# Attention in units of all eight heads, with the row maxima subtracted on GpSimd and one exponential of the transposed scores

## The chip, the cores and the metric

The kernel runs on one core of a Trainium2 chip. Its time is the device time of one execution in microseconds (us). The core has five engines that run their own instruction streams and meet at semaphores: TensorE (PE in the profile, with PEld for its weight loads), VectorE (DVE), ScalarE (ACT), GpSimd (POOL) and SyncE (SP), which issues most of the transfers (DMA). Inputs and outputs lie in HBM, tiles in SBUF, and products of TensorE in PSUM, which GpSimd cannot read.

## The reference

Windowed attention, and behind it an expert layer in which a greedy routing gives each of 8 experts 576 of the 4608 tokens. The change concerns the attention alone, and some constants of the routing.

```python
# q, k, v: (8 batches, 8 heads, 576 tokens, 64)
scores = (q @ k^T) / 8
mask   = 0 <= query - key < 64          # a query sees itself and 63 keys before it
scores = where(mask, scores, -1e9)
scores = scores - max(scores, axis=-1)
attn   = exp(scores) / (sum(exp(scores)) + 1e-9)
x      = (attn @ v)                      # 4608 tokens x (8 heads * 64) = the experts' input
logits = x @ w_gate                      # 8 numbers for each token: greedy choice, 576 tokens for each expert
out[tokens of e] = relu(x[tokens of e] @ w1[e]) @ w2[e]
```

## The kernel before, in words

Tokens are cut into blocks of 64 queries, nine for each batch; a block needs only the 128 keys of its own block and the one before it. Two blocks that follow each other (`a` = 0, 1) make a unit `m` of 128 queries, so there are 36 units, and a unit can reach over the end of a batch. A step of the loop at line 248 works on half a unit: four of the eight heads (`g` = 0, 1), 72 half-units in all, in a pipeline that is written out by hand. A half-unit goes through these stages, one step apart:

- `qk` (line 116): 16 products of TensorE, 64 rows by 64 columns each, into the two PSUM tiles `Sp` of this `g`. Behind them VectorE makes for each head one instruction (line 135) that adds the mask (an SBUF tile) to the PSUM scores, writes the result, negated and scaled, to `st`, and keeps its minimum in `mx`; a second small instruction (DVE_READ_ACCUMULATOR) writes that minimum out. Between the four heads stand the pieces of `norm` of the half-unit four steps back.
- `sm` (line 141): four exponentials on ScalarE, one for each head, since each head's maximum goes in as the per-row bias.
- `tr` (line 148): four 128x128 transposes on TensorE into the PSUM tile `Tp`, and one copy by ScalarE to `pt`.
- `pv` (line 164): 16 products of TensorE, 128 rows by 64 columns each, `pt` times the values, into `Op`. The value tile has 73 columns for each head: 64 values, 8 columns of the head's gate logits, and one column of ones that gives the row sum.
- `norm` (line 177): VectorE adds 1e-9 to the row sums (line 203), takes the reciprocal (204), and scales the gate columns (188) and the values (198). After every fourth unit it sums the gate logits over the heads (192).

Blocks with an even number need keys in an order that the value tile `VO` doesn't have on its partitions; `even` (line 109) copies two halves of each into `VE`, on GpSimd (the first two on VectorE). The gate columns come from products of `vt` with the gate's weights, made for each batch in two parts: `gate_mm` on TensorE, `gate_cp` on ScalarE, `gate_tr` (transposes) on TensorE, `gate_out` on VectorE (lines 80 to 107), which writes them into `VO` and so waits until `v` of that batch has landed.

The order on each engine is the order in which the code is written, and the table `at` says in which step the gate's pieces, the even blocks and the loads of a later batch are put. TensorE's order in a step is `qk(s)`, `tr(s-2)`, `pv(s-3)`, then gate work. All inputs and stores of the attention go through SP's queue, in order; the loads of batches 0 and 1 come first, that of batch b in the middle of batch b-2. Finished units `x` are held back (up to 16) and stored to `xs` later. Between the steps VectorE also runs pieces of the routing: `setup` builds its constants, one or three pieces for each step, and `late` makes each token's best choice once its logits are there. The routing's rounds and the experts follow when the attention is over, and are the same in both kernels.

Of the kernel before, what the change touches and what calls it, by code (L numbers as in the profile page):

```python
# [9 lines left out]
FT = mybir.dt.float32  # L10
# [16 lines left out]
HOLD = 16  # L27
# [3 lines left out]
def attention(ctx, tc, c, q, k, v, vt, gate, xs, L, choices, setup, counters):  # L31
# [48 lines left out]
    def gate_mm(b, i0, i1):  # L80
        if not i0:
            VS[b] = [None, wk.tile([128, S], FT, name="vs", bufs=2)]
        pv = VS[b][0] = ps.tile([128, 512], FT, name="pvt", bufs=1)
        for p in range(HP):
            nc.tensor.matmul(pv[32 * p:32 * p + 32, :64 * (i1 - i0)], wgbd[:, p, :],
                             VT[b][:, p, 64 * i0:64 * i1], start=True, stop=True)
# [2 lines left out]
        nc.scalar.activation(VS[b][1][:, 64 * i0:64 * i1], VS[b][0][:, :64 * (i1 - i0)], AF.Copy)  # L89

    def gate_tr(b, i0, i1):
        pt = VS[b][0] = ps.tile([128, 512], FT, name="pvt", bufs=1)
        for n, j in enumerate(range(i0 // 2, (i1 + 1) // 2)):
            w = 128 if j < 4 else 64
            nc.tensor.transpose(pt[:w, 128 * n:128 * n + 128], VS[b][1][:, 128 * j:128 * j + w], c["ident"])

    def gate_out(b, i0, i1):
        pt = VS[b][0]
        j0, j1 = i0 // 2, i1 // 2
        n = j1 - j0  # L100
        nc.vector.tensor_copy(VO[b][:, j0:j1, :, 64:72],
                              pt[:, :128 * n].rearrange("p (j h g) -> p j h g", j=n, h=8)[:, :, :, :8])
        if i1 % 2:
            nc.vector.tensor_copy(VO[b][0:64, 4, :, 64:72],
                                  pt[:64, 128 * n:128 * n + 128].rearrange("p (h g) -> p h g", h=8)[:, :, :8])
        if not i0:
            VE[b] = ld.tile([128, 4, H, VW], FT, name="VE")

    def even(b, j, eng):

        eng.tensor_copy(VE[b][0:64, j], VO[b][64:128, j])
        eng.tensor_copy(VE[b][64:128, j], VO[b][0:64, j + 1])

    PT_, PB, ST, OP_ = {}, {}, {}, {}

    def qk(m, g, old):
        Sp = [t[g] for t in SP]
# [12 lines left out]
        st = wk.tile([128, 4, 128], FT, name="st")  # L130
        mx = wk.tile([128, 4], FT, name="mx")
        nrm = norm(*old) if old else []
        for h in range(4):

            nc.vector.tensor_tensor_reduce(st[:, h, :], Sp[h % 2][:, h // 2], mk, scale=-0.125, scalar=3.0e38,  # L135
                                           op0=OP.add, op1=OP.min, accum_out=mx[:, h:h + 1])
            if nrm:
                nrm.pop(0)()
        ST[m, g] = (st, mx)

    def sm(m, g):
        st, mx = ST.pop((m, g))
        pe = wk.tile([128, 4, 128], FT, name="pe")
        for h in range(4):
            nc.scalar.activation(pe[:, h, :], st[:, h, :], AF.Exp, bias=mx[:, h:h + 1], scale=-1.0)  # L145
        PB[m, g] = pe

    def tr(m, g):
        Tp = ps.tile([128, 4, 128], FT, name="Tp", bufs=1)
        pe = PB.pop((m, g))  # L150
        for h in range(4):
# [25 lines left out]
    def norm(m, g):  # L177

        Op = OP_.pop((m, g))
        r = wk.tile([128, 4], FT, name="r")  # L180
        if g == 0:
            XT[0] = wk.tile([128, H, D], FT, name="x", bufs=HOLD + 4)
            if m % 4 == 0:
# [13 lines left out]
        def values():  # L197
            nc.vector.tensor_tensor(x[:, 4 * g:4 * g + 4], Op[:, :, 0:64],  # L198
                                    r[:, :, None].to_broadcast([128, 4, 64]), OP.mult)
            if g:  # L200
                stores.append((m, x))

        return [lambda: nc.vector.tensor_scalar(r, Op[:, :, 72], 1e-9, None, op0=OP.add),
                lambda: nc.vector.reciprocal(r, r), gates, values]

    for b in range(2):
        for i in PARTS:
# [12 lines left out]
        load_qk(b, *ALL)  # L220
        load_v(b, *ALL)

    seq = [(m, g) for m in range(36) for g in range(2)]
    n = len(seq)
# [17 lines left out]
    last = []  # L242

    def store(m, x):
        nc.sync.dma_start(xs[128 * m:128 * m + 128], x.rearrange("p h d -> p (h d)"))

    for s in range(n + 4):
        old = seq[s - 4] if 4 <= s else None
        if s < n:
            qk(*seq[s], old)  # L250
        else:
            rs, inv, gates, values = norm(*old)

            for f in (rs, inv, values, gates) if s < n + 2 else (rs, inv, gates):
                f()
            if s >= n + 2:
                last.append(values)
            while late:
                late.pop(0)()
        if 1 <= s < n + 1:  # L260
            sm(*seq[s - 1])

        if stores and (len(stores) > HOLD or s > LOADED):
            store(*stores.pop(0))
        if 2 <= s < n + 2:
            tr(*seq[s - 2])
        if 3 <= s < n + 3:
            pv(*seq[s - 3])
        for f, a in at.get(s, []):
            f(*a)  # L270
        if late:
            late.pop(0)()
        if s > 3:
            for _ in range(3 if s < 10 else 1):
                next(setup, None)
    for f in last:
        f()
    for m, x in stores:
        store(m, x)

# [59 lines left out]
ND = 15  # L340
# [7 lines left out]
class Routing:  # L348


    def __init__(self, ctx, tc, c, V):
# [14 lines left out]
        t("G0", [128, NJ, ND], BF)  # L366
        t("cw", [128, E])
        t("dg", [128, ND], I32)
        t("lane", [128, 1])
        t("rows", [128, 1], U32)  # L370
        self.setup = self.constants(c["jp"], t)
# [2 lines left out]
    def counters(self):  # L374
        iota = self.nc.gpsimd.iota
        iota(self.cw, pattern=[[-1, E]], base=E, channel_multiplier=0, allow_small_or_imprecise_dtypes=True)
        iota(self.dg, pattern=[[1, ND]], base=1, channel_multiplier=0)
        iota(self.rows, pattern=[[0, 1]], base=0, channel_multiplier=1)
        iota(self.lane, pattern=[[0, 1]], base=0, channel_multiplier=1, allow_small_or_imprecise_dtypes=True)

    def constants(self, jp, t):
# [13 lines left out]
        for r in range(NR):  # L395
            yield nc.vector.tensor_scalar(tab[:, r], dg, 28 - 4 * r, None, op0=OP.logical_shift_left)
# [8 lines left out]

        diag = t("diag", [128, 4])
        gt = t("gt", [32, 5])
        for k in range(5):

            yield nc.vector.tensor_scalar(gt[:, k:k + 1], jp[0:32, 8 * k:8 * k + 1], 0.0, None, op0=OP.is_le)  # L410
        for q in range(4):
            yield nc.vector.tensor_tensor(diag[32 * q:32 * q + 32], gt[:, 0:4], gt[:, 1:5], OP.subtract)
        self.sq = [t(f"sq{i}", [128, 32]) for i in range(2)]
# [2 lines left out]
            yield nc.vector.memset(x, 0.0)  # L416

        s5 = t("s5", [72, 2, 4, 5], BF)
        for h in range(2):
            for g in range(4):  # L420
                for k in range(2):

                    n = 5 if g < 2 else 4
                    o = 36 * k + 2 * g + h
                    w = t(f"sx{k}", [72, 5])
                    yield nc.vector.tensor_scalar(w[:, 0:n], jp[0:72, o:o + 8 * n - 7:8], 0.0, None, op0=OP.is_equal)
                    if g > 1:

                        yield nc.vector.tensor_scalar(w[:, 4:5], jp[0:72, o + 28:o + 29], 0.0, None, op0=OP.is_equal)
                    if k:  # L430
                        yield nc.vector.tensor_tensor(s5[:, h, g], w0, w, OP.add)
                    w0 = w

        t("st", [128, 5, E])
        self.left = self.st[:, 4]
# [636 lines left out]
```

## Time and profile before

| | us |
|---|---|
| median of 3 runs (lowest, highest) | 666.29 (665.75, 666.87) |
| the profiled execution, time | 664.41 |
| its span, first to last instruction | 662.8 |
| PE busy | 632.9 (95%) |
| DVE busy | 442.9 (67%) |
| ACT busy | 363.5 (55%) |
| POOL busy | 186.9 (28%) |

The span has three parts: attention up to 162 us (TensorE's first instruction of the routing starts at 162.12 us), the routing's first expert up to about 195 us, and the experts' products. A PE time of 95% is not read as a full TensorE: the ends of pipelined products are modelled, so the distance between the starts of products tells more than their busy time. Times from starts of rows are used below for that reason.

### The profile page before, as it was taken

How to read it: one execution, taken by the hardware profiler on the slowest of the kernel's cores; microseconds unless marked ns; L12 is line 12 of the kernel's file. 1: busy time of each engine (PE TensorE's matmuls, PEld its weight loads, DVE VectorE, ACT ScalarE, POOL GpSimd, SP SyncE). 2: the span in 40 equal slices, each digit the busy share in tenths (PEclk: the TensorE clock that was granted, in tenths of full speed). 3: DMA queues.
4: the chain of work that ended last, by engine and by line, in shares of the span. 5: the costliest groups of instructions: out<-in, count | busy, mean ns of one | idle time of the engine just before them, and what ended most of it. 6: DMA issues, size and time to landing. Idle time of an engine off the chain costs nothing. (4 is left out here: it accounts for less than half of the span.)

```text
span 662.8 us, 16953 instructions
## 1 busy us (share of the span) xinstructions
PE 632.9 (95%) x6383; PEld 533.5 (80%) x6383; DVE 442.9 (67%) x2246; ACT 363.5 (55%) x734; POOL 186.9 (28%) x218
## 2 busy tenths in 40 slices
PE   7999999998569999999999999999999999999995
PEld 6667777776449878987997898799789879989984
DVE  5878898888787766884886688488668852202300
ACT  5788998887046247527724652762465277256310
POOL 0433233330052024206202420620252063052211
PEclk8999999999579999999999999999999999999999
DMA  9999988921068369739766982976697399939701
GB/s 303 349 373 375 373 317 310 388 90 67 19 204 214 69 202 241 183 75 292 196 117 231 218 194 66 284 195 116 230 213 184 83 282 273 232 98 219 143 25 47
DMA packets 50097, 134.10 MB, mean 202 GB/s; under 512 B 4696, under 2 KB 10968, under 8 KB 50016
## 3 DMA queue, kind: packets, MB, share of 16 engines
q0 software_dynamic: 15280, 52.98, 35.8%
q1 hardware_dynamic: 34192, 79.52, 33.6%
q8 instruction: 50, 0.82, 0.5%
q10 hardware_dynamic: 544, 0.52, 0.2%
q14 instruction: 31, 0.25, 0.1%
HBM read 82.15 MB, written 18.87 MB: 152 GB/s over the span
## 5 line engine op out<-in xcount | busy, mean ns | idle before, releaser
L952 POOL DMA_INDIRECT out<-ot,idx x40 | 41.1, 1026 | 296.0 <-DVE ab L630 96.7
L901 ACT ACTIVATE hh<-h 128x256 fp32r<-128x256 f32 (+1 forms) x128 | 52.1, 408 | 103.6 <-PE h L929 102.6
L972 PE MATMUL o<-wh,hl 128*128 128x512 f32 x256 | 102.2, 399 | 0.0
L972 PE MATMUL o<-wl,hh 128*128 128x512 f32 x256 | 101.9, 398 | 0.0
L972 PE MATMUL o<-wh,hh 128*128 128x512 f32 x256 | 100.5, 393 | 0.0
L929 PE MATMUL h<-xh,wl 128*128 128x256 f32 (+1 forms) x512 | 94.4, 299 | 0.0
L145 ACT ACTIVATE pe<-st,mx 128x128 f32<-128x128 f32 x288 | 91.2, 391 | 3.2 <-DVE mx L135 3.2
L135 DVE CUSTOM_DVE_ANT_0 st<-Sp,mask 128x128 f32<-128x128 f32 x288 | 78.8, 277 | 20.8 <-PE Sp L126 14.5
L929 PE MATMUL h<-xh,wh 128*128 128x256 f32 (+1 forms) x512 | 91.5, 299 | 0.7 <-ACT xh L857 0.7
L929 PE MATMUL h<-xl,wh 128*128 128x256 f32 (+1 forms) x512 | 91.1, 297 | 0.5 <-DVE xl L861 0.5
L906 DVE SCALAR_TENSOR_TENSOR hl<-h,hh 128x256 fp32r<-128x256 f32 x128 | 53.2, 416 | 42.1 <-ACT hh L901 41.5
L929 PEld LDWEIGHTS h<-xh,wh 128*128 128x128 f32 x512 | 75.6, 189 | 1.6 <-ACT xh L857 0.8
L929 PEld LDWEIGHTS h<-xh,wl 128*128 128x128 f32 x512 | 76.4, 189 | 0.2
L929 PEld LDWEIGHTS h<-xl,wh 128*128 128x128 f32 x512 | 75.5, 189 | 0.8 <-DVE xl L861 0.7
L812 ACT ACTIVATE wh<-st 128x1024 fp32r<-128x1024 f32 x64 | 67.2, 1050 | 4.6 <-DMA st<-w 4.5
L821 ACT ACTIVATE wl<-wh 128x1024 fp32r<-128x1024 f32 x61 | 64.5, 1057 | 1.2
L823 POOL DMA_DIRECT2D wl<-st x61 | 57.1, 1248 | 16.0 <-ACT wl L821 14.4
L972 PEld LDWEIGHTS o<-wl,hh 128*128 128x128 f32 x256 | 48.1, 188 | 9.3
L972 PEld LDWEIGHTS o<-wh,hh 128*128 128x128 f32 x256 | 48.2, 188 | 9.1
L972 PEld LDWEIGHTS o<-wh,hl 128*128 128x128 f32 x256 | 48.3, 189 | 8.8
L861 DVE TENSOR_TENSOR xl<-tp,xh 128x512 fp32r<-128x512 f32 (+1 forms) x40 | 25.0, 633 | 44.8 <-ACT xh L857 44.5
L173 PE MATMUL Op<-VO,pt 128*64 128x73 f32 x640 | 52.4, 233 | 0.4 <-DVE x L198 0.3
(178 smaller groups left out, 1111.3 us busy)
## 6 DMA issues: line engine op xcount, KB each, us to landing
wl<-st POOLq DMA_DIRECT2D x61, 512.0 KB
st<-w SPq DMA_DIRECT2D x60, 512.0 KB, 6.8
xs<-x SPq DMA_DIRECT2D x36, 256.0 KB, 5.2
VO<-v SPq DMA_DIRECT2D x6, 1168.0 KB, 18.1
VT<-vt SPq DMA_DIRECT2D x6, 1152.0 KB, 11.5
Q<-q SPq DMA_DIRECT2D x6, 1152.0 KB, 11.6
K<-k SPq DMA_DIRECT2D x6, 1152.0 KB, 16.4
VO<-v SPq DMA_DIRECT2D x4, 584.0 KB, 12.0
```

The source lines that it names most:

```text
L135: nc.vector.tensor_tensor_reduce(st[:, h, :], Sp[h % 2][:, h // 2], mk, scale=-0.125, scalar=3.0e38, op0=OP.add, op1=OP.min, accum_out=mx[ ...
L145: nc.scalar.activation(pe[:, h, :], st[:, h, :], AF.Exp, bias=mx[:, h:h + 1], scale=-1.0)
L173: nc.tensor.matmul(Op[64 * a:64 * a + 64, h, :], pt[:, h, 64 * a:64 * a + 64], vv[a][:, 4 * g + h, :], start=True, stop=True)
L812: nc.scalar.activation(hi, st[i], AF.Copy)
L821: nc.scalar.activation(lo, hi.bitcast(FT), AF.Copy, scale=-1.0)
L823: nc.gpsimd.dma_start(lo.bitcast(FT), st[i], accum_op=OP.add)
L861: nc.vector.tensor_tensor(xl[:, :, r], t[:, :, :n], xh[:, :, r].bitcast(FT), OP.subtract)
L901: nc.scalar.activation(hh[:, f, c0:c1], h, AF.Relu)
L906: nc.vector.scalar_tensor_tensor(t, h[:, a - c0:b - c0], 0.0, hh[:, f, a:b].bitcast(FT), op0=OP.max, op1=OP.subtract)
L929: nc.tensor.matmul(h, wv[:, cc, 128 * (f % 2):128 * (f % 2) + 128], xt[:, cc, c0:c1], start=(k == 0), stop=(k == 11))
L952: nc.gpsimd.indirect_dma_start(out=self.out, out_offset=IndirectOffsetOnAxis(ap=idx[0:m, a:a + 1], axis=0), in_=ot[0:m], in_offset=None)
L972: nc.tensor.matmul(o, ht[:, f, 128 * a:128 * a + 128], wt[:, 512 * (f % 2):512 * (f % 2) + 512], start=(k == 0), stop=(k == 23))
```

## The change

A step now works on a whole unit: 36 steps and two to drain. TensorE's order in a step is `qk(s)` of both halves, `tr(s-1)` of both, `pv(s-2)` of both, then gate work. The four exponentials of a half-unit and the copy of its transposes go. In their place GpSimd subtracts the maxima from `st`, in place, in one instruction for four heads; TensorE transposes the differences, and ScalarE takes one exponential of 128x512 as it moves them from PSUM. ScalarE also adds 1e-9 to the row sums, copies the gate columns, and copies the even blocks. `Tp` has two buffers, which the gate's tiles share (`bank()`). Constants of the routing that took 45 small VectorE instructions now take 4, with index tiles that GpSimd writes at the start.

```diff
+    def bank():
+        return ps.tile([128, 512], FT, name="Tp")
...
-        pv = VS[b][0] = ps.tile([128, 512], FT, name="pvt", bufs=1)
+        pv = VS[b][0] = bank()
...
-        nc.vector.tensor_copy(VO[b][:, j0:j1, :, 64:72],
+        nc.scalar.activation(VO[b][:, j0:j1, :, 64:72],
...
-    def even(b, j, eng):
-
-        eng.tensor_copy(VE[b][0:64, j], VO[b][64:128, j])
-        eng.tensor_copy(VE[b][64:128, j], VO[b][0:64, j + 1])
-
-    PT_, PB, ST, OP_ = {}, {}, {}, {}
-
-    def qk(m, g, old):
+    def even(b, j, early):
+
+        for d, e in ((slice(0, 64), j), (slice(64, 128), j + 1)):
+            a = VE[b][d, j], VO[b][64 - d.start:128 - d.start, e]
+            if early:
+                nc.vector.tensor_copy(*a)
+            else:
+                nc.scalar.activation(*a, AF.Copy)
...
     def sm(m, g):
+        st, mx = ST[m, g]
+        nc.gpsimd.tensor_tensor(st, st, mx[:, :, None].to_broadcast([128, 4, 128]), OP.subtract)
+
+    def tr(m, g):
+        Tp = bank().rearrange("p (h q) -> p h q", h=4)
         st, mx = ST.pop((m, g))
-        pe = wk.tile([128, 4, 128], FT, name="pe")
         for h in range(4):
-            nc.scalar.activation(pe[:, h, :], st[:, h, :], AF.Exp, bias=mx[:, h:h + 1], scale=-1.0)
-        PB[m, g] = pe
-
-    def tr(m, g):
-        Tp = ps.tile([128, 4, 128], FT, name="Tp", bufs=1)
-        pe = PB.pop((m, g))
-        for h in range(4):
-            nc.tensor.transpose(Tp[:, h, :], pe[:, h, :], c["ident"])
-        pt = wk.tile([128, 4, 128], FT, name="pt")
-        nc.scalar.activation(pt, Tp, AF.Copy)
+            nc.tensor.transpose(Tp[:, h, :], st[:, h, :], c["ident"])
+        pt = wk.tile([128, 4, 128], FT, name="pt", bufs=4)
+        nc.scalar.activation(pt, Tp, AF.Exp, scale=-1.0)
         PT_[m, g] = pt
...
-        return [lambda: nc.vector.tensor_scalar(r, Op[:, :, 72], 1e-9, None, op0=OP.add),
-                lambda: nc.vector.reciprocal(r, r), gates, values]
+        nc.scalar.activation(r, Op[:, :, 72], AF.Copy, bias=1e-9)
+        return [lambda: nc.vector.reciprocal(r, r), gates, values]
...
-        s0 = 9 * (b - 1) + (6 if b < 4 else 7)
-        for i, s in zip(PARTS, ((1, 5), (7, 11))[b] if b < 2 else (s0, s0 + 2)):
+        s0 = (9 * (b - 1) + (6 if b < 4 else 7)) // 2
+        for i, s in zip(PARTS, ((0, 2), (3, 5))[b] if b < 2 else (s0, s0 + 2)):
...
-                    put(s + 1, even, b, j, nc.gpsimd if b or j > 1 else nc.vector)
+                    put(s + 1 + max(0, j - 1), even, b, j, not b and j < 2)
...
-        put(9 * (b - 2) + 5, load_all, b)
+        put((9 * (b - 2) + 5) // 2, load_all, b)
...
+    def small(s):
+        if late:
+            late.pop(0)()
+        if s > 1:
+            for _ in range(2 if s < 5 else 1):
+                next(setup, None)
...
+    for s in range(n + 2):
         if s < n:
+            fs = [qk(s, g) for g in range(2)]
+            for g in range(2):
+                for h in range(4):
+                    fs[g](h)
+                    if not g and h in (1, 2):
+                        small(s)
+                sm(s, g)
...
+            for g in range(2):
+                tr(s - 1, g)
+        if 2 <= s:
+            for g in range(2):
+                pv(s - 2, g)
+            nrm = [norm(s - 2, g) for g in range(2)]
+            for inv, gates, values in nrm:
+                for f in (inv, gates, values) if s < n + 1 else (inv, gates):
+                    f()
...
+        for _ in range(1 if 2 * s < LOADED else 2):
+            if stores and (len(stores) > HOLD or 2 * s > LOADED):
+                store(*stores.pop(0))
```

The places below show what stands on three engines in the middle of the attention. Line numbers of the changed kernel differ from those of before. The first place is TensorE, two half-units of before: `Sp` are the scores of `qk`, `Tp` the transposes, `Op` the products with the values, and each "..." leaves out more products of the same kind.

```order
L126 MATMUL Sp_93<-K,Q 64x128
L126 MATMUL Sp_95<-K,Q 64x128
...
L152 MATMUL Tp<-ident,pe 128x128 [waits Activation_49]
L152 MATMUL Tp<-ident,pe 128x128 x3
L173 MATMUL Op<-VO,pt 64x73 [waits DVE_49]
L173 MATMUL Op<-VO,pt 64x73 x7
L126 MATMUL Sp_94<-K,Q 64x128
L126 MATMUL Sp_96<-K,Q 64x128
...
L152 MATMUL Tp<-ident,pe 128x128 [waits Activation_49]
L152 MATMUL Tp<-ident,pe 128x128 x3
L173 MATMUL Op<-VE,pt 64x73 [waits DVE_49,Pool_49]
```

The same engine in the changed kernel, one whole unit:

```order
L133 MATMUL Sp_95<-K,Q 64x128 [waits DVE_49]
L133 MATMUL Sp_97<-K,Q 64x128 [waits DVE_49]
...
L133 MATMUL Sp_96<-K,Q 64x128 [waits DVE_49]
L133 MATMUL Sp_98<-K,Q 64x128 [waits DVE_49]
...
L155 MATMUL Tp<-ident,st 128x128 [waits Activation_49,Pool_49]
L155 MATMUL Tp<-ident,st 128x128 x3
L155 MATMUL Tp<-ident,st 128x128 [waits PE_49,Activation_49,Pool_49]
L155 MATMUL Tp<-ident,st 128x128 x3
L176 MATMUL Op<-VO,pt 64x73 [waits DVE_49]
L176 MATMUL Op<-VE,pt 64x73
...
L176 MATMUL Op<-VO,pt 64x73 [waits DVE_49]
```

The work is the same; the kinds change three times in a unit, where they changed six times. The transposes now wait for GpSimd, and the scores have a wait for VectorE of their own. The second place is VectorE, a half-unit of before with the pieces of `norm` between the heads:

```order
L135 ISA st,mx<-Sp_94,mask_138 128x128 [waits PE_49,Activation_49]
L135 ISA mx 128x1
L203 TENSOR_SCALAR r<-Op 128x4
L135 ISA st,mx<-Sp_96,mask_138 128x128 [waits PE_49]
...
L204 RECIPROCAL r<-r 128x4 [waits DVE_49]
...
L188 TENSOR_TENSOR l<-Op,r 128x32 [waits DVE_49]
...
L198 TENSOR_TENSOR x<-Op,r 128x256
L449 TENSOR_TENSOR oh<-L,m 128x32
L429 TENSOR_SCALAR sx_1519<-jp 72x1
```

The same engine in the changed kernel, from the second half of a unit to the first scores of the next:

```order
L142 ISA st,mx<-Sp_96,mask_140 128x128 [waits PE_49,Pool_49]
L142 ISA mx 128x1
L142 ISA st,mx<-Sp_98,mask_140 128x128 [waits PE_49]
...
L207 RECIPROCAL r<-r 128x4 [waits Activation_49]
L191 TENSOR_TENSOR l<-Op,r 128x32 [waits DVE_49,PE_49]
L201 TENSOR_TENSOR x<-Op,r 128x256
L207 RECIPROCAL r<-r 128x4 [waits Activation_49]
...
L142 ISA st,mx<-Sp_95,mask_140 128x128 [waits PE_49,Pool_49]
```

The scores now stand together, and the pieces of `norm` follow each other behind them and wait for ScalarE, with the next unit's scores behind. The third place is ScalarE in the changed kernel, the step in which the gate columns of batch 2 are written (`pt` the exponentials, `r` the row sums, `VO` the gate columns, `VE` the even blocks); before, ScalarE had only `pe`, `pt` and `vs`:

```order
L157 ACTIVATE pt<-Tp 128x512 [waits PE_49] x2
L206 ACTIVATE r<-Op 128x4 [waits DVE_49,PE_49] x2
L119 ACTIVATE VE<-VO 64x584
L119 ACTIVATE VE<-VO 64x584 [waits Activation_49]
L104 ACTIVATE VO<-Tp 128x16x8 [waits DMAHW0_49,PE_49]
L119 ACTIVATE VE<-VO 64x584 [waits Activation_49]
L119 ACTIVATE VE<-VO 64x584
L157 ACTIVATE pt<-Tp 128x512 [waits PE_49] x2
```

The write of the gate columns, with its wait for a transfer, moved from VectorE to ScalarE, and the next exponentials stand behind it.

## Rows read from the trace of the kernel before

**Rows 1.** Windows: span, busy us (count) of PE, PEld, DVE, ACT, POOL; PEclk; DMA share; GB/s.

```profile
13.00:81.00 68.00, 65.34 (x1197) 47.40 (x1198) 58.18 (x448) 56.76 (x163) 21.64 (x31) 1.00 1.06 368
81.00:100.00 19.00, 19.00 (x360) 13.92 (x357) 16.54 (x131) 16.71 (x48) 5.39 (x8) 1.00 0.89 324
```

**Rows 2.** Timeline of PE, one half-unit (start us, us from first start to last end).

```profile
109.65 0.67 PE L126 MATMUL Sp<-K,Q 64*64 64x128 f32 x16
110.25 0.66 PE L152 MATMUL Tp<-ident,pe 128*128 128x128 f32 x4
110.83 0.28 PE L173 MATMUL Op<-VE,pt 128*64 128x73 f32 x1
...
110.95 0.23 PE L173 MATMUL Op<-VE,pt 128*64 128x73 f32 x1
...
111.33 0.22 PE L173 MATMUL Op<-VE,pt 128*64 128x73 f32 x1
...
111.50 0.67 PE L126 MATMUL Sp<-K,Q 64*64 64x128 f32 x16
```

**Rows 3.** Timeline of PE, the same half-unit cut off after 12 scores and 3 transposes.

```profile
109.65 0.56 PE L126 MATMUL Sp<-K,Q 64*64 64x128 f32 x12
...
110.25 0.55 PE L152 MATMUL Tp<-ident,pe 128*128 128x128 f32 x3
```

**Rows 4.** Timeline of PE near the start, two transposes and the gate's transposes behind them.

```profile
10.32 0.63 PE L152 MATMUL Tp<-ident,pe 128*128 128x128 f32 x2
10.75 0.42 PE L95 MATMUL pvt<-ident,vs 128*128 128x128 f32 x1
```

**Rows 5.** Windows of that stretch, columns as in rows 1.

```profile
9.00:11.40 2.40, 2.40 (x26) 1.74 (x30) 0.93 (x8) 1.95 (x6) 0.00 (x0) 0.52 1.07 369
```

**Rows 6.** Timeline of DVE, the gate columns of three batches ([idle before <-releaser]).

```profile
45.84 0.29 DVE L101 COPY VO<-pvt 128x128 f32<-128x128 f32 x1 [2.54 <-DMA VO<-v]
...
103.11 0.29 DVE L101 COPY VO<-pvt 128x128 f32<-128x128 f32 x1
...
121.84 0.29 DVE L101 COPY VO<-pvt 128x128 f32<-128x128 f32 x1
```

**Rows 7.** Timeline of DVE, four scores at the start, and norm's pieces at the end.

```profile
6.08 0.29 DVE L135 CUSTOM_DVE_ANT_0 st<-Sp,mask 128x128 f32<-128x128 f32 x1 [2.05 <-PE Sp L126]
...
6.72 0.29 DVE L135 CUSTOM_DVE_ANT_0 st<-Sp,mask 128x128 f32<-128x128 f32 x1
...
158.89 0.18 DVE L204 RECIPROCAL r<-r 128x4 f32<-128x4 f32 x1
159.10 0.42 DVE L198 TENSOR_TENSOR x<-Op,r 128x256 f32<-128x256 f32 x1
159.45 0.18 DVE L188 TENSOR_TENSOR l<-Op,r 128x32 f32<-128x32 f32 x1
159.54 0.18 DVE L455 TENSOR_TENSOR one<-w,best 128x32 bf16<-128x32 bf16 x1
```

**Rows 8.** Timeline of DVE and POOL, instructions of the one beside copies of the other.

```profile
89.53 0.70 POOL L112 COPY VE<-VO 64x584 f32<-64x584 f32 x1 [2.12 <-DVE VO L101]
89.62 0.63 DVE L431 TENSOR_TENSOR s<-sx,sx 72x5 bf16<-72x5 f32 x1
...
91.00 0.67 POOL L112 COPY VE<-VO 64x584 f32<-64x584 f32 x1
91.04 0.27 DVE L135 CUSTOM_DVE_ANT_0 st<-Sp,mask 128x128 f32<-128x128 f32 x1
...
95.11 0.16 DVE L431 TENSOR_TENSOR s<-sx,sx 72x5 bf16<-72x5 f32 x1
```

**Rows 9.** Groups of instructions of ACT and POOL, by form (busy us, mean ns).

```profile
L154 ACT ACTIVATE pt<-Tp 128x512 f32<-128x512 f32 x72 | 42.7, 593 | 9.6 <-PE Tp L152 6.4
...
L111 POOL COPY VE<-VO 64x584 f32<-64x584 f32 x30 | 20.2, 675 | 85.2 <-issue 32.0 <-DVE VO L101 29.3 <-DMA xs<-x 12.4
```

**Rows 10.** Timeline of PE, the end of the attention (L527 is the routing).

```profile
156.37 0.67 PE L126 MATMUL Sp<-K,Q 64*64 64x128 f32 x16
...
162.12 0.95 PE L527 MATMUL rps<-one,G 128*15 128x8 bf16 x32
```

More of the change, by code (lines that the diff above doesn't have):

```diff
@@ L91, in gate_tr @@
     def gate_tr(b, i0, i1):
-        pt = VS[b][0] = ps.tile([128, 512], FT, name="pvt", bufs=1)
+        pt = VS[b][0] = bank()
         for n, j in enumerate(range(i0 // 2, (i1 + 1) // 2)):
@@ L129, in qk, with scores @@
         mk = c["mask"][tuple(kinds)]
-        st = wk.tile([128, 4, 128], FT, name="st")
-        mx = wk.tile([128, 4], FT, name="mx")
-        nrm = norm(*old) if old else []
-        for h in range(4):
+        st = wk.tile([128, 4, 128], FT, name="st", bufs=4)
+        mx = wk.tile([128, 4], FT, name="mx", bufs=4)
+        ST[m, g] = (st, mx)
+        def scores(h):
             nc.vector.tensor_tensor_reduce(st[:, h, :], Sp[h % 2][:, h // 2], mk, scale=-0.125, scalar=3.0e38,
                                            op0=OP.add, op1=OP.min, accum_out=mx[:, h:h + 1])
-            if nrm:
-                nrm.pop(0)()
-        ST[m, g] = (st, mx)
+        return scores
     def sm(m, g):
+        st, mx = ST[m, g]
+        nc.gpsimd.tensor_tensor(st, st, mx[:, :, None].to_broadcast([128, 4, 128]), OP.subtract)
+    def tr(m, g):
+        Tp = bank().rearrange("p (h q) -> p h q", h=4)
         st, mx = ST.pop((m, g))
-        pe = wk.tile([128, 4, 128], FT, name="pe")
         for h in range(4):
-            nc.scalar.activation(pe[:, h, :], st[:, h, :], AF.Exp, bias=mx[:, h:h + 1], scale=-1.0)
-        PB[m, g] = pe
-    def tr(m, g):
-        Tp = ps.tile([128, 4, 128], FT, name="Tp", bufs=1)
-        pe = PB.pop((m, g))
-        for h in range(4):
-            nc.tensor.transpose(Tp[:, h, :], pe[:, h, :], c["ident"])
-        pt = wk.tile([128, 4, 128], FT, name="pt")
-        nc.scalar.activation(pt, Tp, AF.Copy)
+            nc.tensor.transpose(Tp[:, h, :], st[:, h, :], c["ident"])
+        pt = wk.tile([128, 4, 128], FT, name="pt", bufs=4)
+        nc.scalar.activation(pt, Tp, AF.Exp, scale=-1.0)
         PT_[m, g] = pt
@@ L179, in norm @@
         Op = OP_.pop((m, g))
-        r = wk.tile([128, 4], FT, name="r")
+        r = wk.tile([128, 4], FT, name="r", bufs=4)
         if g == 0:
@@ L221, in load_all @@
         load_v(b, *ALL)
-    seq = [(m, g) for m in range(36) for g in range(2)]
-    n = len(seq)
+    n = 36
     at = {}
@@ new lines, in attention @@
+    for s in range(n + 2):
+        if s < n:
+            fs = [qk(s, g) for g in range(2)]
[5 more added lines that the diff above has]
+                sm(s, g)
+        if 1 <= s < n + 1:
+            for g in range(2):
[7 more added lines that the diff above has]
+                    f()
+            if s >= n:
+                while late:
+                    late.pop(0)()
+            if s == n + 1:
+                for inv, gates, values in nrm:
+                    values()
@@ L269, in attention @@
         for f, a in at.get(s, []):
             f(*a)
[L271 to L277, printed above, removed]
+        for _ in range(1 if 2 * s < LOADED else 2):
+            if stores and (len(stores) > HOLD or 2 * s > LOADED):
+                store(*stores.pop(0))
     for m, x in stores:
@@ L368, in __init__ @@
         t("dg", [128, ND], I32)
+        t("sh", [128, NR], I32)
+        t("v5", [72, 2, 4, 5], I32)
         t("lane", [128, 1])
@@ L377, in counters @@
         iota(self.dg, pattern=[[1, ND]], base=1, channel_multiplier=0)
+        iota(self.sh, pattern=[[-4, NR]], base=28, channel_multiplier=0)
+        iota(self.v5, pattern=[[1, 2], [2, 4], [8, 5]], base=0, channel_multiplier=-1)
+        iota(self.v5[:, :, 2:4, 4], pattern=[[1, 2], [2, 2]], base=32, channel_multiplier=-1)
         iota(self.rows, pattern=[[0, 1]], base=0, channel_multiplier=1)
@@ L394, in constants @@
         tab = t("tab", [128, NR, ND], I32)
-        for r in range(NR):
-            yield nc.vector.tensor_scalar(tab[:, r], dg, 28 - 4 * r, None, op0=OP.logical_shift_left)
+        yield nc.vector.tensor_tensor(tab, dg[:, None, :].to_broadcast([128, NR, ND]),
+                                      self.sh[:, :, None].to_broadcast([128, NR, ND]), OP.logical_shift_left)
         yield nc.vector.tensor_scalar(tab[:, 0, 0:7], tab[:, 0, 0:7], -1, None, op0=OP.bitwise_xor)
@@ L407, in constants @@
         gt = t("gt", [32, 5])
-        for k in range(5):
-            yield nc.vector.tensor_scalar(gt[:, k:k + 1], jp[0:32, 8 * k:8 * k + 1], 0.0, None, op0=OP.is_le)
+        yield nc.vector.tensor_scalar(gt, jp[0:32, 0:33:8], 0.0, None, op0=OP.is_le)
         for q in range(4):
@@ L418, in constants @@
         s5 = t("s5", [72, 2, 4, 5], BF)
[L419 to L432, printed above, removed]
+        w5 = t("w5", [72, 2, 4, 5])
+        yield nc.vector.tensor_scalar(w5, self.v5, 0.0, None, op0=OP.is_equal)
+        yield nc.vector.scalar_tensor_tensor(s5, self.v5, -36.0, w5, op0=OP.is_equal, op1=OP.add)
         t("st", [128, 5, E])
```

27 lines of the change are left out of this document (5 added, 22 removed).

## The prediction

> **What bounds the kernel now.** I read the windows by stretch first, then TensorE's timeline inside one half-unit, then VectorE, GpSimd and ScalarE beside it, and last the start and the end of the attention. The attention ends on TensorE at 162.1 us [rows 10]. From 81 us on TensorE is busy for 19.00 of 19.00 us, VectorE for 16.54 and ScalarE for 16.71 [rows 1]: TensorE is the bound, and the other two are close behind it.
>
> How full is it really? A half-unit takes 111.50 - 109.65 = 1.85 us from scores to scores: 0.60 us for the 16 scores, 0.58 for the four transposes, 0.67 for the 16 value products [rows 2]. Inside a kind the products follow each other faster. Four more scores (they run four at a time) add 0.67 - 0.56 = 0.11 us, one more transpose 0.66 - 0.55 = 0.11 [rows 2, 3]; a pair of value products starts every (111.33 - 110.95) / 6 = 0.063 us [rows 2]. So the work fills 0.44 + 0.44 + 0.51 us, and 0.16 + 0.14 + 0.16 = 0.46 us of each half-unit are pauses, one at each change of kind. With 72 half-units that is 33 us.
>
> Is the pause the price of a change of kind, or of any new group with a semaphore? Near the start the transposes of the gate follow those of the scores: the same shape, another tile, a wait of their own. From the third transpose to the gate's first are 10.75 - 10.32 = 0.43 us for two, 0.215 each [rows 4]; the granted clock is 0.52 there [rows 5], the 1.2 GHz level, and 0.215 is twice the 0.11 of the 2.4 GHz level. There is no pause. And the scores of before, which wait for nothing in the order, have it. So it goes with the kind.
>
> **The change, part by part.**
>
> *TensorE.* The products are the same. A unit had six changes of kind and now has three: 3.70 - 0.46 = 3.24 us for a unit (1.04 scores, 1.02 transposes, 1.18 values). Over all 36 units that would be 16.6 us, the upper end of the gain.
>
> *The first nine units gain little.* Up to 81 us the DMA engines are full (share 1.06 at 368 GB/s) [rows 1]. The gate columns of batch 2 are written at 45.84 us, after a wait of 2.54 us for that batch's values [rows 6]. The transfers before it have the same order, so I take the same landing. This wait now stands on ScalarE, with the next exponentials behind it and, through the gate's tile in the shared `Tp` bank, TensorE's transposes. So TensorE comes to step 9 early, stops at its second four transposes, and goes on at 46.2 (45.84 plus the copy's 0.29 and a handoff).
>
> *From there.* The rest of step 9: 0.5 + 1.18, and 0.68 for the gate's products (an estimate, a third of a batch's gate work): 2.4 us. Steps 10 to 35: 26 x 3.24 = 84.2. Gate work takes what a batch's 121.84 - 103.11 = 18.73 us [rows 6] leave over nine half-units of 1.85: 2.1 us. Five batches and a transposition are 10.9. The two draining steps: 1.02 + 2 x 1.18, and 0.9 in which TensorE waits for the last subtraction (by the times below it ends 4.6 us after the last unit's scores begin, and TensorE is there after 3.7): 4.3. The sum is 46.2 + 2.4 + 84.2 + 10.9 + 4.3 = 148.0, against 162.1: 14.1 us less, before the losses below.
>
> *VectorE* loses the additions of 1e-9 and the gate copies, but also its interleaving. Four scores by themselves take (6.72 - 6.08) / 3 = 0.213 us each [rows 7], so eight take 1.70. The pieces of `norm` now depend on each other directly: 0.21 from the reciprocal to the next, 0.35 for the values, 0.09 for the gate columns [rows 7], 0.65 for a half, 1.30 for a unit. With the sums over heads and the choices (0.3, estimated from the 0.16 to 0.18 of the smallest rows) a unit takes 3.3 us. That is above 3.24 and below 3.24 + 2.1 / 4.5 = 3.70, TensorE's mean with the gate work. Units without gate work lose up to 0.1 us: 1 us in all.
>
> *GpSimd's subtraction* is in no row. From below: a copy of 584 columns takes 675 ns [rows 9], so 512 columns 0.59 us. From above: if two operands and a write were read one after the other, three times that, 1.8 us. I take 1.2, twice the copy for two operands. GpSimd is in a loop: end of the values of unit u, ScalarE's addition with its handoffs (0.35), VectorE's second half of `norm` (0.65), four scores with the choices (1.1), two subtractions, the second transposes (0.5), the values of unit u+2 (1.18), and 0.2 for handoffs. That is 4.0 + 2P in two units. With P = 1.2 it is 6.4, just under 2 x 3.24, and costs nothing; with 0.59 likewise; with 1.8 a unit takes 3.8.
>
> *ScalarE* loses the four exponentials of each half-unit. For a unit it now has two exponentials of 0.593 [rows 9], two small additions (between nothing and that 0.593; I take 0.2, near VectorE's smallest), and 8 copies of even blocks for 4.5 units at GpSimd's 0.675 (1.2 for a unit): some 2.8 of 3.7 us. Three steps hold four such copies and a gate copy, some 1 us too many; the additions behind them come late and VectorE waits. The 0.5 to 0.7 us of gate work in the same and the next step hide most of it: 0.5 us lost in all, and up to 3 if none is hidden.
>
> *The rest.* 45 constants become 4; they run before the stop at 46 us or in VectorE's gaps: nothing. The few index instructions of GpSimd stand in front of its first subtractions, also before 46 us: nothing; beyond it they would cost their own length, 1 to 3 us. Stores are as many for each unit and still behind the loads. After the attention all is as before and only starts earlier; ScalarE's additions cost the last `norm` a handoff more, 0.3 us.
>
> Sum: -14.1 + 1.0 + 0.5 + 0.3 = -12.3 us. The execution that I read took 664.41 us for a span of 662.8; by it the new span is 650.5 and the time 652.1. The median of the runs lies 1.9 us above that execution, so the forecast is 666.3 - 12.3 = **654.0 us**.
>
> At one place a rule speaks against this. VectorE's `s` took 0.63 us beside a copy on GpSimd and 0.16 without one, while a score's 0.27 us did not change beside one [rows 8]. The Trainium skill, "SBUF — State Buffer", section "SBUF: two separate sides", says that the two engines share a pair of ports, held for a whole instruction, and that VectorE needs it for two operands in SBUF or in its faster two-port modes. By that rule a subtraction blocks only instructions like `s` (the choices), not the scores, which read one operand from PSUM; the trace agrees, and the sum stands. Were the scores held too, it would be the third rival.
>
> **The rivals.**
>
> *GpSimd is the bound.* The subtraction takes 1.7 to 2.1 us. For it: none has been timed, and it reads a second operand that repeats one number for 128 columns. Against it: the copy's rate would have to fall to a third. At 1.8 a unit takes 3.8 to 3.9 with gate work instead of 3.7: 26 x 0.2 = 5 us of the gain go, **659**. From 2.1 on, where 2.0 + P is before's mean of 4.16, nothing is left.
>
> *The loads are late throughout.* A batch now passes in 16.7 us where it took 18.7. At 324 GB/s [rows 1] that was 6.06 MB a batch with stores, and would be 363 GB/s, right at the 368 at which the engines were full. If batches 3 to 5 come as late as batch 2, 2 us each go: **660**. Against it: after 46 us no wait for a load is in the rows of the gate columns [rows 6].
>
> *The slower side: GpSimd and VectorE exclude each other.* Every score adds a mask from SBUF and `norm` multiplies by `r` from SBUF. If a subtraction held them up, a unit would take 3.3 + 2 x 1.2 = 5.7 us against 4.16 before: 36 x 1.5 = 55 us more, **720**. It is slower as soon as 0.43 us of each subtraction exclude VectorE. For it speaks the 0.63 us of `s`, against it the score beside the copy [rows 8].
>
> *The change doesn't save pauses.* They belong to each group of 16 and not to the kind: a unit stays at 3.70, **666**. Against it: the gate's transposes without a pause [rows 4]. The Trainium skill, "TensorEngine Tiling (Array Packing)", section "Key Properties", says that changing the tiling mode, not just the tile, drains the engine. By that rule this rival has no place; the rows agree.
>
> **How the numbers follow.** The forecast gets 0.65, GpSimd as the bound 0.17 (of it 0.02 slower), late loads 0.07, exclusion 0.05, no saving 0.06. The forecast's own range is 650 (16.6 us, all pauses gone) to 657 (3 us lost in ScalarE's full steps). To hold 8 in 10, the range reaches up to a slow GpSimd and late loads: 650 to 662. About 0.2% (1.3 us) is what can be told from no change. Faster: 0.65 + 0.15 + 0.07 = 0.87; same: 0.06; slower: 0.07.
>
> **What would show it.** TensorE's rows: scores to scores 3.2 to 3.4 us in units without gate work, transposes of both halves without a pause between them; the routing's first product near 149.8 us; gate columns of batch 2 at about 45.8 with a wait for the transfer, now on ScalarE. GpSimd's subtraction near 1.2 us; scores of VectorE still at 0.28 us beside it. It is wrong if TensorE waits for GpSimd in every unit, if the scores lengthen, or if the pauses stay between the two halves of a kind.

## The result and the profile after

The changed kernel takes 660.22 us (median of 4 runs, 659.36 to 661.20) against 666.02 for the kernel before: a ratio of 0.9911, 95% interval 0.9892 to 0.9930, or 5.8 us less. The forecast was 654.0. The execution profiled took 659.36 us, its span 657.7.

The windows of TensorE's two stretches, columns as in [rows 1]:

```profile
46.00:81.00 35.00, 32.30 (x654) 25.84 (x652) 28.27 (x207) 24.69 (x59) 17.41 (x18) 1.00 1.01 363
81.00:100.00 19.00, 18.99 (x390) 14.91 (x383) 16.94 (x119) 14.40 (x33) 9.85 (x10) 1.00 0.84 300
```

From 81 us on TensorE is as full as before and starts 390 products in 19 us where it started 360. From 46 to 81 us, with the DMA engines full, 2.7 us of its time are empty. That is the first sign: the cheaper unit isn't lost, the engine is kept waiting.

TensorE's timeline over one unit without gate work (its first value products only):

```profile
143.75 1.10 PE L133 MATMUL Sp<-K,Q 64*64 64x128 f32 x32
144.78 1.10 PE L155 MATMUL Tp<-ident,st 128*128 128x128 f32 x8
145.81 0.28 PE L176 MATMUL Op<-VO,pt 128*64 128x73 f32 x1
...
146.99 1.10 PE L133 MATMUL Sp<-K,Q 64*64 64x128 f32 x32
```

146.99 - 143.75 = 3.24 us, in parts of 1.03, 1.03 and 1.18: the forecast unit, to 0.01 us, against 3.70 from [rows 2]. GpSimd's subtraction and VectorE's scores, as groups of instructions between 46 and 147 us (busy us, mean ns, idle before):

```profile
L149 POOL TENSOR_TENSOR st<-st,mx 128x512 f32<-128x512 f32 x51 | 52.0, 1040 | 50.4 <-DVE mx L142 34.2 <-PE Tp L155 11.6 <-PE Op L176 4.6
```

```profile
L142 DVE CUSTOM_DVE_ANT_0 st<-Sp,mask 128x128 f32<-128x128 f32 x206 | 48.2, 286 | 1.7 <-PE Sp L133 1.6
```

The subtraction takes 1.04 us (1.2 were taken) and GpSimd waits half of its time; the scores take 0.286 us beside it, as in [rows 8]. Neither is the bound. So where did 6 us go? TensorE stops in three ways that before did not have. First, step 9:

```profile
45.52 0.66 PE L155 MATMUL Tp<-ident,st 128*128 128x128 f32 x4
46.96 0.63 PE L155 MATMUL Tp<-ident,st 128*128 128x128 f32 x4 [0.78 <-ACT VO L104]
...
49.45 0.28 PE L176 MATMUL Op<-VE,pt 128*64 128x73 f32 x1 [0.95 <-issue]
49.92 0.74 PE L88 MATMUL Tp<-VT,wgs 128*32 128x320 f32 x8
50.59 0.45 PE L133 MATMUL Sp<-K,Q 64*64 64x128 f32 x8
```

ScalarE's timeline there shows one cause (the counterpart of [rows 6]):

```profile
44.43 1.40 ACT L119 ACTIVATE VE<-VO 64x584 f32<-64x584 f32 x2
46.52 0.29 ACT L104 ACTIVATE VO<-Tp 128x128 f32<-128x128 f32 x1 [0.69 <-DMA VO<-v]
46.84 1.39 ACT L119 ACTIVATE VE<-VO 64x584 f32<-64x584 f32 x2
48.26 1.09 ACT L157 ACTIVATE pt<-Tp 128x512 f32<-128x512 f32 x2
49.23 0.18 ACT L206 ACTIVATE r<-Op 128x4 f32<-128x4 f32 x1
```

The gate copy waits for the values of batch 2, as forecast, and starts at 46.52 instead of 45.84. Behind it come two copies of an even block (1.39 us), and only then the exponentials that the second value products need; these are done at 49.35, and TensorE goes on at 49.45. At 100 and 136 us the same row of instructions delays steps 23 and 32 by 0.52 us each.

Second, stops in the middle of the scores (products of the unit in step 13, and of the one in step 26):

```profile
61.40 0.44 PE L133 MATMUL Sp<-K,Q 64*64 64x128 f32 x6
62.68 1.03 PE L133 MATMUL Sp<-K,Q 64*64 64x128 f32 x26 [0.84 <-issue]
```

```profile
111.67 0.88 PE L133 MATMUL Sp<-K,Q 64*64 64x128 f32 x23
113.19 0.54 PE L133 MATMUL Sp<-K,Q 64*64 64x128 f32 x9 [0.64 <-issue]
```

"issue" says that no semaphore explains it. A queue of the page, and a window of 0.2 us at 60.1 us, 1.6 us ahead of the first stop, point to a cause:

```profile
q8 instruction: 50, 0.82, 0.5%
```

```profile
DMA packets 36, 0.09 MB, mean 462 GB/s; under 512 B 2, under 2 KB 2, under 8 KB 35
...
q1 hardware_dynamic: 35, 0.08, 101.4%
q8 instruction: 1, 0.02, 34.8%
```

Queue 8 moves 50 packets of 0.82 MB / 50 = 16 KB of instructions. TensorE's records of the execution are 6383 weight loads, 6383 products and 187 others: 259 for each packet. (The Trainium skill, "Trainium Architecture — The Big Picture", section "The software stack", gives an instruction 64 bytes, which makes 256 in 16 KB; the trace agrees with its 259.) Counted from the start, the three long "issue" stops (18.61, 61.57 and 112.28 us) stand behind record 448, 1984 and 4033: 6 and 8 x 256 apart, to one record. And in each, the next product starts 2.58, 2.44 and 2.47 us after a queue 8 packet starts (at 18.22, 60.24 and 110.72). TensorE has run out of instructions; the experiments test this. With the DMA engines full, that packet mostly starts 3 to 5 us after the end of the one before is reached (60.24 after 55.5, 110.72 after 106.8); where they have room it starts at once (138.68 after 138.66).

Why not before? There the same 256 instructions take some 6.9 us (ends at 56.6, 63.3, 70.4 and 77.3), and each packet starts 3.4 us or more before TensorE needs it. Now they take 6.2.

Third, the end (the counterpart of [rows 10]):

```profile
154.42 0.25 PE L176 MATMUL Op<-VO,pt 128*64 128x73 f32 x1 [0.69 <-DVE r L207]
...
155.68 0.25 PE L176 MATMUL Op<-VO,pt 128*64 128x73 f32 x1 [0.52 <-DVE best L452]
...
156.34 0.80 PE L526 MATMUL rps<-one,G 128*15 128x8 bf16 x26
```

The routing starts 162.12 - 156.34 = 5.8 us sooner; 149.8 had been forecast. At the end of the two profiled executions 5.1 us of it are left (spans of 662.8 and 657.7): from the routing's first product on, the changed kernel takes 501.4 us and the one before 500.7, where the forecast let all of this only start earlier. Why is open.

### The profile page after: what moved, and what is told of

Its sections match the earlier page's. It is cut to its first block, busy times and chain, and to the rows that moved or that the text cites. A ratio compares the mean times of both kernels' runs of the same rounds, so it can differ in the third digit from the quotient of the medians.

```text
span 657.7 us, 16919 instructions
## 1 busy us (share of the span) xinstructions
PE 622.0 (95%) x6383; PEld 533.8 (81%) x6383; DVE 433.0 (66%) x2109; ACT 335.6 (51%) x602; POOL 219.2 (33%) x233
## 5 line engine op out<-in xcount | busy, mean ns | idle before, releaser
L149 POOL TENSOR_TENSOR st<-st,mx 128x512 f32<-128x512 f32 x72 | 73.4, 1040 | 73.7 <-DVE mx L142 54.2
L142 DVE CUSTOM_DVE_ANT_0 st<-Sp,mask 128x128 f32<-128x128 f32 x288 | 67.4, 285 | 8.0 <-PE Sp L133 7.7
L866 POOL DMA_INDIRECT xg<-xs,idx x40 | 40.8, 1020 | 34.7 <-DVE eq L709 23.1
```

Of the source, the lines that this page charges most:

```text
L149: nc.gpsimd.tensor_tensor(st, st, mx[:, :, None].to_broadcast([128, 4, 128]), OP.subtract)
L866: nc.gpsimd.indirect_dma_start(out=g[0:n, a], out_offset=None, in_=self.xs, in_offset=IndirectOffsetOnAxis(ap=idx[0:n, a:a + 1], axis=0))
```

## Experiments

Theory A: the queue of ScalarE costs the missing time. Theory B: TensorE's late instructions do, and they are late because of the loads. The third candidate is that the gain of the kinds is smaller than it looks. "Stops" below are the distances of over 0.3 us between the starts of two products at the ends of instruction packets in steps 10 to 34; these steps take 96.4 us in the changed kernel, from its scores of step 10 to those of step 35.

**No even copies.**

```diff
...
-            vv.append(VO[b][:, i // 2] if (i % 2 or i == 0) else VE[b][:, i // 2 - 1])
+            vv.append(VO[b][:, min(i // 2, 3)])
...
-                    put(s + 1 + max(0, j - 1), even, b, j, not b and j < 2)
+                    pass
```

> Leaves out the copies of even blocks (value products of even blocks read the odd alignment, so other numbers come out; the count of products is the same). Theory A, ScalarE's queue (two pairs of copies of 0.69 us each in front of the gate copy, the exponentials and the row-sum additions) holds TensorE: steps 9, 22 and 23, 31 and 32 lose their waits, 1.2 + 0.7 + 0.7, and step 27 and the last steps up to 0.9: about -3.5 us against the changed kernel, 656.7. Theory B, waits for TensorE's own instructions and the drain took the missing gain: -1 us at most, 659.2 or more, and the stops of about 1 us inside the scores stay.

656.95 us, ratio 0.9863 (0.9832 to 0.9895). Steps 23 and 32 take 3.91 each (4.43), and from TensorE's wait in step 9 to the scores of step 10 it takes 2.4 us (46.63 to 49.05), as forecast. But the stops stay: 0.87, 0.32, 0.42, 0.59 and 0.36, 2.6 us in all, for 2.4 in the changed kernel. Both theories hold a part.

**Even copies spread.**

```diff
-                    put(s + 1 + max(0, j - 1), even, b, j, not b and j < 2)
+                    put(s + 1 + (j - 1 if j else int(b > 1)), even, b, j, not b and j < 2)
```

> The first pair of even copies of batches 2 to 7 moves one step later, so that no step from 9 on has four. Theory A (ScalarE's queue): steps 9, 23 and 32 recover, -1.2 - 0.5 - 0.5 = -2.2 us, 658.0. Theory B (instruction waits and the drain): within 0.7 us of the changed kernel's 660.2, because the stop in step 9 is also one in which TensorE waits for instructions.

660.16 us, ratio 0.9906 (0.9874 to 0.9938): no difference. Step 10 starts 0.9 us sooner (49.68), and then the stops are 3.8 us (one of 1.58) where they were 2.4. Six steps, each the one behind a moved copy, also take 0.13 us more. What ScalarE gave back, the instructions and the moved copies took.

**One copy of each pair on GpSimd.**

```diff
+            elif d.start:
+                nc.gpsimd.tensor_copy(*a)
```

> One copy of each pair of even blocks goes to GpSimd (0.68 us), the other stays on ScalarE (0.69 us). Theory (ScalarE's queue): steps 23 and 32 lose their 0.52 us each and step 9 up to 1.2: -1.5 us, 658.7, less what the instruction stops take back (up to 1). Rival: GpSimd, with 2 x 1.02 of subtraction a unit and one or two copies in some steps, comes late and TensorE waits for the subtraction: 660 to 663.

657.03 us, ratio 0.9876 (0.9859 to 0.9892). The copies there take 0.666 us, and GpSimd isn't late: steps 23 and 32 take 3.91. Steps 18, 22 and 31 are 0.2 us shorter as well: there, too, the second half's transposes had waited for ScalarE (the eight transposes of step 18 take 1.09 us here, 1.29 in the changed kernel). The stops are 3.1 us.

**Only TensorE's order undone.** In the loop over steps, the scores, transposes, value products and `norm` of four heads come before those of the other four:

```diff
-            fs = [qk(s, g) for g in range(2)]
-            for g in range(2):
...
+        for g in range(2):
+            if s < n:
+                fs = qk(s, g)
...
+            if 1 <= s < n + 1:
+                tr(s - 1, g)
+            if 2 <= s:
+                pv(s - 2, g)
```

> The subtraction, the one exponential of the transposed scores and ScalarE's new work stay; only TensorE's order goes back to half-units (16 scores, 4 transposes, 16 value products, then the other four heads). Theory: the three pauses of 0.16, 0.14 and 0.16 us come back in each of the two halves, 3.70 us for a unit without gate work, +0.46 x 36 = +16 us at most; the instruction stops (2.5 us) and some waits are covered by it: 668 to 675. Rival, that the gain came from the cheaper exponentials or VectorE and not from the kinds: 660 to 662.

665.98 us, ratio 1.0006 (0.9996 to 1.0016): the time of before, and 2 us under what was expected. A half-unit without gate work (its first value product only):

```profile
146.87 0.67 PE L133 MATMUL Sp<-K,Q 64*64 64x128 f32 x16
...
148.05 0.28 PE L176 MATMUL Op<-VE,pt 128*64 128x73 f32 x1
...
148.72 0.45 PE L133 MATMUL Sp<-K,Q 64*64 64x128 f32 x8
```

148.72 - 146.87 = 1.85 us, as in [rows 2]. So the pauses belong to the changes of kind, the grouping is the whole gain, and the new softmax and ScalarE's new work by themselves give nothing. (The whole units with the softmax of before were not run.) In steps 10 to 34 no instruction stop is left; 256 instructions last 6.4 to 7.5 us there (ends at 57.0, 63.4, 70.5, 77.5, 84.0, 90.5, 97.9).

**The packets moved.**

```diff
+    for _ in range(64):
+        nc.tensor.matmul(x[0:32, 0, 0:8], z[:, 0:32], z[:, 0:8], start=True, stop=True)
```

> 64 tiny products more in front of the first scores (128 instructions, half of one 16 KB instruction packet; about 2 us, ahead of the first loads' end). Theory B: the place of the long stops goes with the packet and not with the work: no stop at the products where units 13 and 26 stopped, and stops, if any, 64 products earlier or later (counted from the start of the program at the same instruction). Rival, that a key or query load or a buffer holds unit 13: the stop stays at its product. The time as a whole is open, 658.5 to 662, since the new places may be better or worse.

658.43 us, ratio 0.9881 (0.9850 to 0.9913). The unit of step 13 runs through, and a stop stands in another unit's scores (the value products end just ahead of it):

```profile
62.56 1.10 PE L135 MATMUL Sp<-K,Q 64*64 64x128 f32 x32
...
77.41 0.87 PE L135 MATMUL Sp<-K,Q 64*64 64x128 f32 x21
79.16 0.65 PE L135 MATMUL Sp<-K,Q 64*64 64x128 f32 x11 [0.88 <-issue]
```

It is the only long one left in these steps. The stop goes with the packet and not with a load or a buffer of the unit.

**Queries and keys loaded for two batches only.**

```diff
-        load_qk(b, *ALL)
+        Q[b], K[b] = Q[1], K[1]
```

> Queries and keys of batches 2 to 7 are not loaded: the units use those of batch 1 (other numbers, the same instructions). DMA is no longer full from about 25 us on. Theory B (TensorE's instructions land late behind the loads, 2.44 us and more after their packet starts): the stops of 1.08, 0.87 and 0.3 us go, and the values of batch 2 land some 5 us sooner, so that the stop before step 9 (1.1 us) goes too: -3.5 us or more, 656.7 or less. Rival (ScalarE's queue alone): the stops inside the scores stay, only the 1.1 us go: 659.

656.83 us, ratio 0.9855 (0.9824 to 0.9887). The DMA share from 46 to 81 us falls to 0.48, and both long stops go; step 9 takes 4.44 us. One stop of 0.86 us is left, at 117.43, in a stretch with a DMA share of 0.79. So most of the stops go with the loads, and half of the loads is enough for one at times; when, the mean share of 20 us doesn't tell (with still fewer loads, below, the same stretch has 0.84 and no stop).

**Batch 2 in two parts**, alone, with GpSimd's copies, and with the packets moved as well.

```diff
-        load_vt(b, *ALL)
-        load_qk(b, *ALL)
-        load_v(b, *ALL)
+        for i in PARTS if b == 2 else (ALL,):
+            load_vt(b, *i)
+            load_qk(b, *i)
+            load_v(b, *i)
```

> The load of batch 2 comes in two parts (first four blocks, then five) as those of batches 0 and 1 do, so that the values for the first part land some 6 us sooner; all else as in the changed kernel. Theory: the stop before the second transposes of step 9 (1.05 us, behind the gate copy that waits for the values) goes, and no other takes its place: -1.0 to -1.5 us, 658.7 to 659.2. Rival: the DMA engines are full, the second part is late for step 10 or an instruction stop takes the place: within 0.5 us of 660.2.

> As e9_parts, and one copy of each pair of even blocks on GpSimd as in e7_pool. If the two are independent: e7_pool's ratio of 0.9876 less 1.0 to 1.5 us more, 655.5 to 656 at a before of 665.2. If TensorE only meets more instruction stops: e7_pool's time.

> As e10_pool_parts, with the 64 tiny products of e5_shift in front, which move the ends of the instruction packets by 64 products. Theory: long stops come where an end lies among the scores, just behind the value products, so that 128 instructions pass in 2.2 us; with the shift fewer ends lie there, and the stops after step 10 fall from some 3 us to 1.5 to 2: -1 to -1.5 us against e10_pool_parts, 654.5. Rival: the faster TensorE runs into as many stops at the new places: no difference.

They took 660.85 (ratio 0.9918, 0.9904 to 0.9931), 657.62 (0.9862, 0.9844 to 0.9880) and 658.54 us (0.9883, 0.9868 to 0.9898). The wait for values goes in all three, step 9 takes 5.52, 4.73 and 3.91 us instead of 6.10, and the time doesn't follow: all three miss what the theory expected. The stops grow in its place to 3.4, 4.2 and 5.2 us. In the last, whose step 9 waits for nothing, this one among the scores shows it:

```profile
77.63 0.86 PE L137 MATMUL Sp<-K,Q 64*64 64x128 f32 x19
79.67 0.48 PE L137 MATMUL Sp<-K,Q 64*64 64x128 f32 x9 [1.17 <-issue]
```

In these runs an earlier TensorE only meets its instructions earlier; that this holds wherever the loads fill the DMA engines isn't shown, since GpSimd's copies alone did gain 2 to 3 us. My rule that fewer packet ends among the scores would help on top of this was wrong.

**Most loads left out**, alone and with GpSimd's copies.

```diff
-        load_vt(b, *ALL)
-        load_qk(b, *ALL)
+        VT[b], Q[b], K[b] = VT[1], Q[1], K[1]
         load_v(b, *ALL)
```

> Of batches 2 to 7 only the values are loaded; queries, keys and the transposed values are those of batch 1 (other numbers, the same instructions; a fourth of the loads is left). If TensorE's instructions come late because they stand behind the loads, no packet's end stops TensorE after 30 us: steps 10 to 34 take 25 x 3.24 + 11.8 of gate work + 1.0 in steps 23 and 32 = 93.9 us (96.4 in the changed kernel), and step 9 loses the 1.1 us in which it waits for values: -3.6 us or more, 656.6 or less. If they come late whatever the loads, the stops stay: 659.

> The same, with one copy of each pair of even blocks on GpSimd as in e7_pool: neither ScalarE's queue nor the loads can hold TensorE. Steps 10 to 34 take 25 x 3.24 + 11.8 = 92.8 us and step 9 no more than 4: -5 to -6 us against the changed kernel, 654 to 655, the time that was forecast without these two. If a third cause holds TensorE, 656 or more.

656.18 us (ratio 0.9848, 0.9824 to 0.9872) and 652.84 us (0.9808, 0.9782 to 0.9833). Steps 10 to 34 take 94.2 and 92.0 us (93.9 and 92.8 were expected), with no stop at a packet's end. The windows of the second, and its unit of step 13:

```profile
46.00:81.00 35.00, 35.00 (x732) 28.53 (x726) 32.07 (x232) 21.10 (x56) 24.63 (x29) 1.00 0.29 95
81.00:100.00 19.00, 19.00 (x398) 15.37 (x397) 17.25 (x122) 11.80 (x32) 13.63 (x16) 1.00 0.43 143
```

```profile
59.76 1.10 PE L135 MATMUL Sp<-K,Q 64*64 64x128 f32 x32
```

With a DMA share of 0.29 in place of 1.01, TensorE is full for all 35 us. Without these two causes the change takes the forecast time, near enough: the routing starts at 150.58 us (149.8). In part this is luck, since the wait for the values of batch 2, which the forecast had counted, is gone here too, and the drain is as late as in the changed kernel.

**The drain**, alone and with GpSimd's copies: the last unit's value products go to the banks of the transposes, and the values of unit 34 are scaled at the end.

```diff
-        Op = po.tile([128, 4, VW], FT, name="Op")
+        Op = po.tile([128, 4, VW], FT, name="Op") if m < 35 else bank()[:, 0:4 * VW].rearrange(...)
...
-                for f in (inv, gates, values) if s < n + 1 else (inv, gates):
+                for f in (inv, gates, values) if s < n else (inv, gates):
```

> The last unit's value products write to the banks of the transposes, so that they needn't wait until unit 34's result is read, and the values of unit 34 are scaled after the gate columns of unit 35. Theory: the two stops of 0.92 and 0.74 us inside the last value products go and VectorE ends 0.7 us sooner: -0.8 us, 659.4, with the first routing product near 154.8 (156.34). Rival: the end is set by ScalarE's and VectorE's chain for the last unit and not by the banks: no difference.

> The two changes before together: the sum of the two if they are independent, about -2.3 us, 657.9; less if an instruction stop takes the place of the waits removed.

661.90 us (ratio 0.9954, 0.9937 to 0.9971) and 657.56 us (0.9880, 0.9864 to 0.9897). The first is a miss; the second lands near its expected time by luck, since the drain costs where it should gain, and GpSimd's copies (657.03 alone) gain more than had been counted for them. Both stops in the last value products go, but the routing's first product now waits for the values that are read from a bank of the transposes:

```profile
159.61 1.06 PE L528 MATMUL rps<-one,G 128*15 128x8 bf16 x36 [4.25 <-DVE x L201]
```

It stands at 159.61 instead of 156.34. What the drain is worth stays open.

The best of these that does the whole computation is GpSimd's share of the copies, with batch 2 in parts or without: 8 to 9 us under the kernel before. The intervals of the two overlap.

## Why the prediction was half right

Right: the bound, the price of a change of kind, the unit of 3.24 us, GpSimd off the bound, the scores not held, the first nine units gaining little, the direction. The range held too, but by luck: its part above 657 was kept for a slow GpSimd (659) and for late loads (660), and neither came. The subtraction takes 1.04 us, and no gate copy behind that of batch 2 waits for a transfer; what came late behind the loads were TensorE's instructions. VectorE's loss of 1.0 us did not come: the units of steps 16, 25 and 34, without gate work, take 3.23 to 3.24 us.

Wrong: the size, 5.8 us for 12.3. By the prediction's own steps, to the routing's first product at 156.34 instead of 149.8:

| step | forecast | measured | late |
|---|---|---|---|
| scores of step 10 begin (46.2 + 2.4) | 48.6 | 50.59 | 2.0 |
| 25 units of 3.24 | 81.0 | 81.0 | 0 |
| gate work, steps 10 to 34 | 10.9 | 11.0 | 0.1 |
| VectorE's and ScalarE's losses | 1.5 | 1.8 (ScalarE alone) | 0.3 |
| TensorE without instructions, steps 13, 14, 26, 27 | none | 2.5 | 2.5 |
| step 35 and the drain (3.24 + 4.3 + 0.3) | 7.8 | 9.35 | 1.5 |

The measured column of the third to fifth row is what steps 10 to 34 take over 25 x 3.24: 96.4 - 81.0 = 15.4. The gate work is what is left of it without most loads and with GpSimd's copies (92.0 - 81.0). ScalarE's 1.8 are 0.5 in steps 23 and 32 each and 0.2 in steps 18, 22, 27 and 31 each; the 2.5 are by how much steps 13, 14, 26 and 27 are longer than in the run with the values only. Of the 2.0 us in the first row, 0.7 are the later landing of the values (46.52 for 45.84, why is open), and 1.2 are the stop in step 9.

The step that failed is "Steps 10 to 35: 26 x 3.24": it lets TensorE run at the rate of its products wherever no listed wait stands in its way, and no term asks whether the instructions themselves arrive at that rate. The runs showed a fifth of the rate's gain lost there in the changed kernel (2.5 of 25 x 0.46 = 11.5 us), and more as soon as other waits are removed. The profile before had the data for it: queue 8, full DMA engines, and packets that start 3.4 us before they are needed, where 2.2 to 2.8 turned out to be the least.

The second failure is a size, and it weighs as much. "Three steps hold four such copies ... 0.5 us lost in all, and up to 3 if none is hidden": without the copies the time falls by about 3.3 us. The 0.5 rested on gate work that would hide them; in the steps above it did not, and in step 9 they stand behind a wait for a transfer and nothing hides them. There ScalarE's exponentials and an instruction packet (started at 46.87, 2.58 us ahead of 49.45) end together, so the 1.2 us have two causes, and by these times either alone would have held most of them. With the copies spread 0.4 us stayed.

The third is the drain: the last value products wait for `norm` of the unit before, which holds their banks. The sum counted a wait for the subtraction only.

## What to carry to other kernels

When an engine's work gets denser, its instruction stream does too. Read the instruction queue of the page: how many instructions a packet holds, how long they last, and how far ahead of its end the next packet starts while the DMA engines are full; that distance is the room for speeding up. And before work is put on a queue that is "only half busy", look at what stands behind it in the steps that hold most of it, with its waits for transfers.

## What was not expected of the hardware

A packet of TensorE's instructions was usable 2.2 to 2.8 us after it started, in every stop counted here, and with full DMA engines it started up to 5.9 us after the end before it (46.87 after 41.0 in the changed kernel). The Trainium skill, "DMA: Bandwidth & Descriptors", section "Queues, rings and completion order", has the engines go round the queues by packets; by that such a wait should be short. When a packet is asked for is in no record, so the runs don't decide it.

A stop can cost more than its length. In the run with the packets moved, TensorE was idle for 1.87 us in step 9, and the granted clock behind it was the 1.2 GHz level, 0.51 for 3 us (the row of TensorE's timeline, and windows with the columns of [rows 1]):

```profile
47.87 1.08 PE L157 MATMUL Tp<-ident,st 128*128 128x128 f32 x4 [1.87 <-ACT VO L106]
```

```profile
44.00:47.80 3.80, 2.00 (x40) 1.42 (x38) 2.93 (x23) 1.88 (x5) 2.19 (x3) 1.00 1.04 315
47.80:51.00 3.20, 3.13 (x36) 2.70 (x36) 0.53 (x3) 2.50 (x5) 0.63 (x1) 0.51 1.05 390
```

The step took 7.50 us instead of 6.10. In the changed kernel the idle time of 0.78 us at the same place left the clock at 1.00. The length of a stop doesn't settle it: the changed kernel's idle 1.9 us from 18.9 to 20.8 us left the clock at 1.00 (20.8 to 22.0), and behind the same stop in the run with the values only it was 0.50 (22.6 to 24.0).
